# DeltaNet feeding a GELU layer pair on one core: chunk 0's state update tied to chunk 1's first joins, ScalarE's exponents, squares and scalings pinned, chunk 2's tail brought forward

## The chip, the cores and the metric

The kernel runs on one core of a Trainium2 chip. The metric is the device time of one execution in microseconds (us); smaller is better. Times inside an execution are counted from the start of the profiled span. A core has a matrix engine (TensorE, PE in the profile, with its weight loads as PEld), VectorE (DVE), ScalarE (ACT), GpSimd (POOL) and a queue of its own for issuing DMAs (SyncE, SP). Each of them works through its own list of instructions in order, and they wait for each other by semaphores.

## The reference

```python
B, H, S, D = 4, 8, 768, 48               # inputs q, k, v, beta
k_n = k / (norm(k) + 1e-06)
state = zeros(B, H, D, D)
for t in range(S):
    y[:, :, t] = q[:, :, t] @ state      # per head
    v_old = state^T k_n[:, :, t]
    state = state + beta[:, :, t] * outer(k_n[:, :, t], v[:, :, t] - v_old)
x = y.transpose(0, 2, 1, 3).reshape(B * S, H * D)     # 3072 x 384
h = x @ w_in                                          # 384 x 2048
g = 0.5 * h * (1.0 + erf(h / sqrt(2)))                # exact GELU
out = g @ w_out                                       # 2048 x 384
```

All data that is computed with is float32; the two weight matrices arrive as 64-bit floats.

## The kernel before

**Chunks.** The sequence of 768 tokens is cut into 12 chunks of 64 tokens. A chunk has two units (a = 0 and 1) of two batches each, so a unit's tokens of two batches fill the 128 partitions. Inside a chunk the recurrence is written as products of small matrices: the gram matrix of the keys (`products`, `grams`), the inverse of a triangular 64x64 matrix for each of 32 heads, computed on VectorE on 32x32 diagonal blocks by elimination (`eliminate_steps`, a chain of L443 and L445 pairs) and joined to 64x64 on TensorE in two levels (`join`, L488; VectorE's L499 writes the first level's result `XM`, ScalarE's L503 the second's), then `against_state` (L603), `solve` (L633, copied out by ScalarE's L639), `use` (L651, the outputs), `update` (L660, the new contribution to the state) and `next_state` (VectorE's L665 adds it to `St`). `read` (L672 by ScalarE for chunks 0 and 1, L674 by VectorE after) gives x, and `turn` transposes x on TensorE (L692 for chunk 1, L695 for the others) and copies it as `xT` (L696). Chunk 1's `turn` adds two parts, y and x, in PSUM. A pair of chunks shares one elimination.

**The layers.** `fc1` (L718) computes one slice f of 128 of the 2048 hidden columns for both units of a chunk, three matmuls, and ScalarE puts the GELU (L720) into `G[:, f]`. For chunks 0 and 1 `fc2` (L731) multiplies G by w_out, four slices f at a time for each unit, and the last group is followed by a copy to `o_sb` (L735) and two output DMAs issued by ScalarE (`send`, L725). From chunk 2 on the second layer takes seven products of half size (L756) with sums on VectorE (`mix`). PSUM holds four kinds of buffers: `dn` (two, of two banks each: psJ, psU, psY, psK, psG, and psH for the first eight slices of chunk 1), `mlp` (two: psH and psO), and the small pool `sq` (psT, psX and, from late in chunk 0's time, one buffer alone).

**The weights.** Each weight is a pair of 32-bit words; VectorE and ScalarE put together the 32-bit float from them, in 16 parts: 0 to 7 are w_in (256 columns, two slices f each), 8 to 15 are w_out (two rows of slices f each). A part takes `begin` on VectorE (L218, cut out the exponent), `exponents` on ScalarE (L223), `mantissas` on VectorE (L228 and L230) and `signed` on VectorE (L235 and L236), and `signed` also fetches a later part into the place that came free. Parts 0 to 2 are decoded in the section that is ordered by hand, the others by the plan.

**What sets the order.** The first part of the program, up to `by_hand.close()`, is under a manual schedule of all engines: there each engine's order is the order of the calls. It ends, for chunk 0, with the decoding of parts 0, 1 and 2 woven into `solve`, `use`, `read`, `turn`, `update` and `next_state`. What follows is a list `plan` of pairs of a due time and a function. `at(first, last, steps)` spreads steps between two due times, `emit` sorts all of them by time and calls them. The unit of due time is about one chunk: fc1 and fc2 of chunk c lie between c + 1 and c + 2 (chunk 0 to 2.25, chunk 1 from 2.25). VectorE alone keeps that order; the orders of TensorE, ScalarE, SP and GpSimd come from a scheduler that may move ready instructions around. Two helpers hold instructions in place: `tc.keep_in_program_order(i)` pins one, and `together(...)` chains the TensorE instructions of its steps to one another and to the one before, so that nothing gets between.

Around the change the plan holds: chunk 0's sixteen fc1 slices; the joins of chunk 1's units (`join(0, range(2, 4), level)`), due from 1.02 to 1.1; `sums`, 32 single-head squares with a sum (L291) for chunks 2 and 3, due from 1.08 to 1.5; the decoding of parts 3 to 15 from 0.985 to 1.65; `state_steps(1)` from 1.12 to 1.6; `scale_head` (L329, the values of chunks 2 and 3 scaled head by head on ScalarE, 32 of them) from 2.08 to 2.44; and near the end of chunk 1's layers `state_steps(2)` without its first step from 2.8 to 2.985, and the grams of chunk 4 from 2.8 to 2.9. `prep(4)` (L278, whole squares of the keys on ScalarE) is due at 2.73, and the ones of chunk 5 before 3. Loads of later chunks are issued on SP by `fetch_in` (L96) and `load_blocks` (L134, sixteen small DMAs for a chunk).

Of the kernel before, what the change touches and what calls it, by code (L numbers as in the profile page):

```python
# [12 lines left out]
ACT = mybir.ActivationFunctionType  # L13
# [3 lines left out]
def kernel(  # L17
# [28 lines left out]
    nc = tc.nc  # L46
    B, H, S, D = q.shape
    DM, DF = moe_w_in.shape
    C = 64
    HB = 32  # L50
    NC = S // C
    NP = H // 2
    NA = B // 2
# [15 lines left out]
    def dn(name):  # L69
        return ps.tile([128, 2, 512], F32, tag="dn", name=name)  # L70

    def sq(name, *shape):
        return small[0].tile([128, *shape], F32, tag="sq", name=name)
# [9 lines left out]
    lim = cpool.tile([128, 2], F32)  # L83
# [7 lines left out]
    tiles = {}  # L91
# [7 lines left out]
    for c in range(NC):  # L99
        for a in range(NA):  # L100
            u = tiles[c, a] = Unit()
# [48 lines left out]
    first = [tiles[c, a] for c in range(2) for a in range(NA)]  # L150
# [63 lines left out]
    def begin(n):  # L214
        e = su.tile([128, WG], U32, tag="w_e", name="w_e")
        raw = w_raw.pop(n)
        halves[n] = w_parts[n][0].rearrange("q m n -> q (m n)"), raw[:, :, 0], raw[:, :, 1], e
        nc.vector.tensor_scalar(e, raw[:, :, 1], 20, 0x7FF, op0=ALU.logical_shift_right,  # L218
                                op1=ALU.bitwise_and)

    def exponents(n):
        e = halves[n][3]
        nc.scalar.activation(e, e, ACT.Relu, bias=lim[:, 0:1], scale=float(2 ** 23))  # L223

    def mantissas(n):
        dst, lo, hi, e = halves[n]
        bits = dst.bitcast(U32)
        nc.vector.tensor_scalar(bits, hi, 0xFFFFF, 0x100000, op0=ALU.bitwise_and,  # L228
                                op1=ALU.bitwise_or)
        nc.vector.scalar_tensor_tensor(dst, lo, 2.0 ** -32, bits, ALU.mult, ALU.add)  # L230
# [10 lines left out]
    def decode_steps(first, last):  # L241
        def start_(n):
            begin(n)
            exponents(n)

        steps = [(0.6, start_, first), (1.5, mantissas, first)]
        for n in range(first, last):
            if n + 1 < last:
                steps += [(0.6, start_, n + 1), (1.9, signed, n), (1.5, mantissas, n + 1)]
        return steps + [(1.9, signed, last - 1)]  # L250
# [4 lines left out]
    Ds, Gs, Nus, XMs, gms, ns = {}, {}, {}, {}, {}, {}  # L255
# [27 lines left out]
    def sum_of_squares(u, h):  # L283

        if "both" not in ns:
            n23 = wk.tile([128, 2 * NA, H], F32, tag="n0", name="n0", bufs=1)
            ns[2], ns[3] = n23[:, 0:NA], n23[:, NA:]
            ns["both"] = n23
        if h == 0:
            u.ksq = wk.tile([128, H, D], F32, tag="ksq", name="ksq")  # L290
        nc.scalar.activation(u.ksq[:, h], u.Kn[:, h, 0:D], ACT.Square,  # L291
                             accum_out=ns[u.c][:, u.a, h:h + 1])

    def prep(c):
        us = [tiles[c, a] for a in range(NA)]
# [30 lines left out]
            nc.vector.scalar_tensor_tensor(x if i == 2 else s, s, 0.5, r, ALU.mult, ALU.add)  # L326

    def scale_head(u, h):
        nc.scalar.mul(u.V[:, h], u.V[:, h], ns[u.c][:, u.a, h:h + 1])  # L329

    def scale_v(u, engine=nc.gpsimd):
        engine.tensor_tensor(u.V, u.V, ns[u.c][:, u.a].unsqueeze(2).to_broadcast([128, H, D]),
                                op=ALU.mult)
# [144 lines left out]
    def join(g, ts, level, copy=nc.scalar.copy):  # L478

        xm, zf, off = XMs[g], Zf[g % 2], Gs[g]  # L480
        gm = gms[g].rearrange("q t h -> q (t h)")
        psJ = dn("psJ").rearrange("q b (u n) -> q b u n", n=HB)
        for i, u in enumerate(range(ts[0] * H, (ts[-1] + 1) * H)):
            for p in range(2):
                top = slice(p * C, p * C + HB)
                low_ = slice(p * C + HB, (p + 1) * C)
                rows, to = (top, low_) if level == 0 else (low_, top)
                nc.tensor.matmul(psJ[to, i // (2 * H), i % (2 * H), :],  # L488
                                 lhsT=(xm if level else off)[rows, u, :],
                                 rhs=zf[rows, u, HB:C] if level else xm[rows, u, :],  # L490
                                 start=True, stop=True)
        for i in range(0, len(ts), 2):
            us = slice(ts[i] * H, (ts[min(i + 1, len(ts) - 1)] + 1) * H)
            n = us.stop - us.start
            for p in range(2):
                top = slice(p * C, p * C + HB)
                low_ = slice(p * C + HB, (p + 1) * C)
                if level == 0:
                    nc.vector.tensor_tensor(  # L499
                        xm[low_, us, :], psJ[low_, i // 2, 0:n],  # L500
                        gm[low_, us].unsqueeze(2).to_broadcast([HB, n, HB]), op=ALU.mult)
                else:
                    copy(zf[top, us, HB:C], psJ[top, i // 2, 0:n])  # L503
# [70 lines left out]
    def join_steps(g):  # L574
        a, b = range(NA), range(NA, 2 * NA)
        return [(join_run, g, a, ()), (join_run, g, b, a), (join_run, g, (), b)]
# [79 lines left out]
    def update(u):  # L656
        if u.c < NC - 1:
            for j in range(NP):
                for r, p in QUADS:
                    nc.tensor.matmul(u.psS[HALF[r], p, j, :], lhsT=u.Kp[HALF[p], 2 * j + r, :],  # L660
                                     rhs=u.U[HALF[p], 2 * j + r, :], start=True, stop=True)

    def next_state(u):
        if u.c < NC - 1:
            nc.vector.tensor_tensor(St[:, u.a], St[:, u.a], u.psS, op=ALU.add)  # L665
# [32 lines left out]
    def state_steps(c, first=(), second=()):  # L698
        us = [tiles[c, a] for a in range(NA)]
        steps = [(3.0, together, (against_state, us), *first),  # L700
                 (2.0, together, (solve, us), *second), (3.0, outputs, us)]
        return steps + [(0.5, turn, u) for u in us]


# [128 lines left out]
    def ffn_steps(c):  # L833
        ones = [(1.3, fc1, c, f) for f in range(NF)]
        if c > 1:
            return [(1.3, first_layer, c, f) for f in range(NF)] + [
                (2.6, second_layer, c, n) for n in (1, 5, 2, 6, 4, 7, 3)]
        twos = [(2.7, fc2, tiles[c, a], f, f + 4) for a in range(NA) for f in range(0, NF, 4)]
        if c == 0:
            twos.sort(key=lambda s: s[3])  # L840
            more_ = [(1.3, fc1, 1, f) for f in range(EARLY)]
            return ones + twos[:-2 * NA] + more_[:4] + twos[-2 * NA:-NA] + more_[4:] + twos[-NA:]
        return ones[EARLY:] + twos

    def at(first, last, steps):

        total, done, timed = sum(s[0] for s in steps), 0.0, []
        for w, *step in steps:
            timed.append((first + (last - first) * (done + 0.5 * w) / total, step))
            done += w  # L850
        return timed
# [78 lines left out]
    clear_[0](*clear_[1:])  # L930
    for u in first[NA:]:
        scale_v(u)
    begin(0)
    exponents(0)
    mantissas(0)
    begin(1)
    mantissas(1)
    solve(first[:NA])
    exponents(1)
    signed(0)  # L940
    use(first[:NA])
    for u in first[:NA]:
# [1 line left out]
    signed(1)  # L944
    for u in first[:NA]:
        turn(u)
    for u in first[:NA]:
        update(u)
    begin(2)
    exponents(2)  # L950
    mantissas(2)
    signed(2)
    for u in first[:NA]:
        next_state(u)
    by_hand.close()
    tc.no_sync_barrier()

# [3 lines left out]
    def late():  # L961
# [3 lines left out]
        for a in range(NA):  # L965
# [3 lines left out]
            for c in range(5, NC, 2):  # L969
                tiles[c, a].Kb = Kb  # L970

    plan = [at(c + 1 + 0.25 * (c == 1), c + 2 + 0.25 * (c == 0), ffn_steps(c)) for c in range(NC)]
    plan += [at(0.985, 1.26, decode_steps(3, n_in)), at(1.26, 1.65, decode_steps(n_in, NW)), at(1.66, 1.67, [(1.0, late)])]
    rows1, join1 = eliminate_steps(1), join_steps(1)
    plan += [at(0.98, 0.985, [(1.0, load, 3)]),
             at(1.02, 1.1, [(1.0, join, 0, range(NA, 2 * NA), level) for level in range(2)]),
]
    sums = [(1.0, sum_of_squares, tiles[c, a], h) for c in (2, 3) for a in range(NA) for h in range(H)]
    plan += [at(1.08, 1.5, sums), at(1.51, 1.511, [(1.0, prep, c) for c in (2, 3)]), at(1.65, 1.655, [(1.0, finish_both)]), at(2.97, 2.971, [(1.0, finish, 4)]), at(2.725, 2.726, [(1.0, queries, third)]),
             at(1.12, 1.6, state_steps(1)),  # L980
# [4 lines left out]
             at(2.71, 2.711, [(1.0, subtract, third)]),  # L985
             at(2.7, 2.701, [(1.0, together, join1[1]), (0.0, copy_out, "join", 4)]),
             at(2.75, 2.751, [(1.0, together, join1[2]), (0.0, copy_out, "join", 4)]),
             at(2.8, 2.985, state_steps(2)[1:]),
             at(2.73, 2.731, [(1.0, prep, 4)]), at(2.8, 2.9, [(1.0, grams, [tiles[4, a] for a in range(NA)])])]
    plan += [at(0.995, 1.0, [(1.0, load_v, 2)]), at(2.98, 2.981, [(1.0, sums_of_w)]), at(3.1, 3.11, [(1.0, last_sum_of_w)])]  # L990
    plan += [at(c - 0.4, c - 0.3, v_steps(c)) for c in range(4, NC)]
    plan += [at(2.08, 2.44, [(1.0, scale_head, tiles[c, a], h)
# [2 lines left out]
    for c in range(4, NC):  # L995
        us = [tiles[c, a] for a in range(NA)]
        t = {4: 1.8, 5: 2.1}.get(c, c - 2.9)
        plan += [at(t, t + 0.01, [(1.0, load_blocks, c, "Kb", k)])]
        t = 3.2 if c == 4 else c - (1.3 if c % 2 == 0 else 0.9)
        plan += [at(t, t + 0.01, [(1.0, load_blocks, c, "Qb", q)])]  # L1000
        t = c - (2.1 if c % 2 == 0 else 2.4) if c > 5 else {4: 2.1, 5: 2.74}[c]
        plan += [at(t, t + 0.01, [(1.0, load_k, c, "Kn")])]
        plan += [at(c - 0.4, c - 0.39, [(1.0, load_k, c, "Kp")])]
        t = {4: 2.76, 5: 2.955}.get(c, c - (1.97 if c % 2 == 0 else 2.49))
        plan += [at(t, t + 0.01, [(1.0, turned_k, u) for u in us])]
        t = c + (0.05 if c % 2 == 0 else -0.34)
# [67 lines left out]
```

## Time and profile before

| | us |
|---|---|
| median of six runs | 659.95 |
| lowest and highest | 659.13, 660.38 |
| the profiled execution's own time | 659.91 |
| its span | 658.2 |
| TensorE busy in the span | 631.7 (96%) |
| VectorE busy | 456.7 (69%) |
| ScalarE busy | 230.5 (35%) |
| GpSimd busy | 80.8 (12%) |

The span is what the profiler records from the first to the last instruction; the profiled execution's own time is 1.7 us longer. In the timeline a row names the start, the duration, the engine, the line and the operation with output and input, how many instructions it stands for, and in brackets the idle time before it and who ended it. A matmul of float32 appears as two records, so the three matmuls of an fc1 slice are six records. Rows that overlap by about 0.1 us on VectorE or ScalarE are back to back: the time from one start to the next is what an operation costs there. TensorE is busy from about 60 us on nearly without a break, and the prefix before that, in which the first units are prepared, takes the rest. The granted clock of TensorE is half of full from 43.48 to 60.52 us and full after.

### The profile page before, as it was taken

What the parts mean: (1) busy time and instruction counts of PE and PEld (TensorE: products, weight loads), DVE (VectorE), ACT (ScalarE), POOL (GpSimd) and SP (SyncE); (2) the same over time, 40 slices, a digit from 0 to 9 for tenths busy, and PEclk for the clock granted to TensorE, in tenths of its full rate; (3) what the DMA queues carried; (4) which work ended last, traced back from release to release, by engine and by line L of the source; (5) the groups of instructions that cost most, each with busy time, mean ns of one, the idle gap of its engine ahead of it and who ended that gap; (6) DMA issues with size and microseconds to landing.
All of it is one profiled execution on the core that took longest, in us unless ns stands there. A gap on an engine that the chain in (4) does not pass through costs nothing.

```text
span 658.2 us, 20461 instructions
## 1 busy us (share of the span) xinstructions
PE 631.7 (96%) x8902; PEld 555.1 (84%) x8902; DVE 456.7 (69%) x941; ACT 230.5 (35%) x625; POOL 80.8 (12%) x82
## 2 busy tenths in 40 slices
PE   6767999999999999999999999999999999999997
PEld 5656777776689989989989989989989989989997
DVE  6999999987789845778845778845778844325022
ACT  3367755614342136232136132136132133131220
POOL 4041300104111011301011300011301010000000
PEclk9986999999999999999999999999999999999999
DMA  9795656302434223520323520212310210100101
GB/s 128 172 268 169 124 145 169 49 1 53 82 40 71 45 36 58 98 41 10 59 34 56 102 38 15 46 17 43 58 21 18 49 14 3 25 2 2 24 1 25
DMA packets 158426, 39.68 MB, mean 60 GB/s; under 512 B 150016, under 2 KB 153216, under 8 KB 158336
## 3 DMA queue, kind: packets, MB, share of 16 engines
q1 hardware_dynamic: 152464, 33.40, 27.0%
q10 hardware_dynamic: 5872, 4.97, 3.3%
q8 instruction: 70, 1.15, 0.7%
q14 instruction: 20, 0.16, 0.1%
HBM read 33.62 MB, written 4.72 MB: 58 GB/s over the span
## 4 chain that ended last, share of the span: by engine, by line
PE 86%; DVE 8%; ACT 2%; DMA 2%; issue 2%; SPq 0%; DVEq 0%
PE psH L718 36%; PE psX L756 12%; PE psY L756 12%; PE psO L731 5%; PE psZ L756 4%; PE psK L603 3%; PE psG L367 3%; PE psJ L529 3%; PE psU L633 2%; PE psY L651 2%; DVE Nu L445 2%; DVE tmp L443 2%; PE psY L660 1%; DMA Kp<-in_k_dram 1%; DVE w_e L235 1%
## 5 line engine op out<-in xcount | busy, mean ns | idle before, releaser
L718 PE MATMUL psH<-xT,w_in_sb 128*128 128x256 f32 x1152 | 258.9, 382 | 2.9 <-ACT G L720 2.3
L718 PEld LDWEIGHTS psH<-xT,w_in_sb 128*128 128x128 f32 x1152 | 216.5, 190 | 34.6 <-ACT G L720 3.8
L720 ACT ACTIVATE G<-psH 128x256 f32<-128x256 f32 x192 | 73.5, 383 | 179.7 <-PE psH L718 161.0
L445 DVE TENSOR_TENSOR Nu<-Nu,tmp 128x30 f32<-128x30 f32 (+9 forms) x180 | 62.4, 347 | 6.2
L443 DVE TENSOR_TENSOR tmp<-Nu 128x30 f32<-128x30 f32 (+9 forms) x180 | 60.6, 337 | 5.0
L696 ACT COPY xT<-psX 128x384 f32<-128x384 f32 x24 | 11.4, 479 | 126.8 <-PE psX L695 126.2
L756 PE MATMUL psX<-w_out_sb,G 128*128 128x192 f32 x320 | 55.8, 328 | 0.0
L756 PE MATMUL psY<-w_out_sb,G 128*128 128x192 f32 x304 | 54.1, 329 | 1.1
L756 PEld LDWEIGHTS psX<-w_out_sb,G 128*128 128x128 f32 x320 | 52.4, 190 | 0.6
L756 PEld LDWEIGHTS psY<-w_out_sb,G 128*128 128x128 f32 x304 | 49.1, 190 | 3.2 <-DVE u L802 3.2
L765 DVE TENSOR_TENSOR S<-G 128x512 f32<-128x512 f32 x20 | 13.8, 691 | 46.4 <-ACT G L720 46.2
L731 PE MATMUL psO<-w_out_sb,G 128*128 128x384 f32 x128 | 44.8, 493 | 0.0
L306 POOL TENSOR_TENSOR n<-n,half 128x16 f32<-128x16 f32 x10 | 29.4, 2940 | 123.1 <-DVE n L281 102.9
L616 DVE TENSOR_TENSOR W<-psK,V 128x384 f32<-128x384 f32 x22 | 12.2, 554 | 33.6 <-ACT y L615 33.6
L731 PEld LDWEIGHTS psO<-w_out_sb,G 128*128 128x128 f32 x128 | 23.3, 190 | 14.0 <-DVE w_out_sb L236 0.5
L639 ACT COPY U<-psU 64x192 f32<-64x192 f32 x96 | 30.1, 313 | 7.5 <-PE psU L633 6.4
L470 POOL MEMSET Zf<- 32x512 f32 x23 | 12.4, 541 | 163.4 <-DVE Zf L458 162.4
L770 DVE TENSOR_TENSOR G<-G 128x512 f32<-128x512 f32 x20 | 13.8, 692 | 25.7 <-PE psX L756 25.7
L674 DVE TENSOR_TENSOR x<-psY,y 64x192 f32<-64x192 f32 x80 | 28.3, 354 | 0.9
L756 PE MATMUL psY<-T,G 128*128 128x192 f32 x160 | 28.2, 329 | 0.0
L756 PE MATMUL psZ<-T,S 128*128 128x192 f32 x160 | 28.1, 329 | 0.0
L756 PE MATMUL psX<-T,G 128*128 128x192 f32 x160 | 28.1, 329 | 0.0
(141 smaller groups left out, 856.2 us busy)
## 6 DMA issues: line engine op xcount, KB each, us to landing
Kp<-in_k_dram SPq DMA_DIRECT2D x76, 96.0 KB, 3.3
w_out_sb<-in_moe_w_in_dram SPq DMA_DIRECT2D x24, 256.0 KB, 4.2
V<-in_v_dram SPq DMA_DIRECT2D x48, 96.0 KB, 3.4
out_dram<-o_sb ACTq DMA_DIRECT2D x46, 96.0 KB, 2.2
w_raw<-in_moe_w_out_dram SPq DMA_DIRECT2D x10, 384.0 KB, 7.3
Zf<-in_moe_w_out_dram SPq DMA_DIRECT2D x6, 384.0 KB, 3.7
Qp<-in_q_dram SPq DMA_DIRECT2D x64, 32.0 KB, 2.2
Qp<-in_q_dram SPq DMA_DIRECT2D x16, 96.0 KB, 4.2
```

Source lines behind the costliest of these rows:

```text
L306: nc.gpsimd.tensor_tensor(flat, flat, half, op=ALU.pow)
L367: nc.tensor.matmul(psG[HALF[p], r, i * NP + j, :], lhsT=u.Kt[rows, p, j, :], rhs=(u.Qt if x else u.Kt)[rows, p, j, :], start=True, stop=True)
L443: nc.vector.tensor_tensor(tmp, nu[:, j + 1:, j:j + 1].to_broadcast([128, n, j]), nu[:, j:j + 1, 0:j].to_broadcast([128, n, j]), op=ALU.mult)
L445: nc.vector.tensor_tensor(nu[:, j + 1:, 0:j], nu[:, j + 1:, 0:j], tmp, op=ALU.add)
L529: nc.tensor.matmul(psJ[HALF[p], k, :], lhsT=(xm if level else off)[rows, us, :], rhs=zf[rows, us, HB:C] if level else xm[rows, us, :], sta ...
L603: nc.tensor.matmul(u.psK[to, x, r, j, :], lhsT=(u.Qt if x else u.Kt)[rows, p, j, :], rhs=St[rows, u.a, p, j, :], start=True, stop=True)
L639: copy(pairs(u.U[HALF[p]], s), u.psU[HALF[p ^ s], p])
L674: nc.vector.tensor_tensor(dst, src, pairs(u.y[HALF[p ^ s]], s), op=ALU.add)
L718: nc.tensor.matmul(psH, lhsT=w_in_sb[:, f // 2, m, f % 2 * 128:(f % 2 + 1) * 128], rhs=xTs[c][:, m, :], start=(m == 0), stop=(m == NM - 1))
L720: nc.scalar.activation(G[:, f, :], psH, ACT.Gelu)
L731: nc.tensor.matmul(u.psO, lhsT=G[:, f, u.a * 128:(u.a + 1) * 128], rhs=w_out_sb[:, f, :], start=(f == 0), stop=(f == NF - 1))
L756: nc.tensor.matmul(ps_, lhsT=lhs[:, f, :], rhs=rhs[:, f, :], start=first and f == 0, stop=f == FH - 1, skip_group_check=not first)
```

## The change

The exponents of parts 3 and 4, the single-head squares and the scalings of single heads are pinned in ScalarE's program order. In the section by hand the decoding of parts 0 and 1 is regrouped: both `begin`, then both `exponents`, then both `mantissas`, all ahead of `solve`. `update` and `next_state` of chunk 0 leave that section and go into the plan, behind chunk 0's first fc1 slices: the updates are tied on TensorE to the first level of chunk 1's joins, and the two `next_state` and the load of chunk 3 follow. The first three slices of fc1 get due times of their own, and the second level of the joins is due at 1.1. Joins of a group's second chunk take their PSUM from the small pool, and `join` does the lower half of the partitions first. `outputs` of chunk 1 is tied together. At the end of chunk 1's layers the steps of `state_steps(2)` get due times one by one (2.79, 2.86, 2.93 and 2.95), and the grams of chunk 4 stand at 2.87.

```diff
     def exponents(n):
         e = halves[n][3]
-        nc.scalar.activation(e, e, ACT.Relu, bias=lim[:, 0:1], scale=float(2 ** 23))
+        i = nc.scalar.activation(e, e, ACT.Relu, bias=lim[:, 0:1], scale=float(2 ** 23))
+        if n in (3, 4):
+            tc.keep_in_program_order(i)
...
-        nc.scalar.activation(u.ksq[:, h], u.Kn[:, h, 0:D], ACT.Square,
-                             accum_out=ns[u.c][:, u.a, h:h + 1])
+        tc.keep_in_program_order(nc.scalar.activation(
+            u.ksq[:, h], u.Kn[:, h, 0:D], ACT.Square, accum_out=ns[u.c][:, u.a, h:h + 1]))
...
     def scale_head(u, h):
-        nc.scalar.mul(u.V[:, h], u.V[:, h], ns[u.c][:, u.a, h:h + 1])
+        tc.keep_in_program_order(
+            nc.scalar.mul(u.V[:, h], u.V[:, h], ns[u.c][:, u.a, h:h + 1]))
...
-        psJ = dn("psJ").rearrange("q b (u n) -> q b u n", n=HB)
+        psJ = dn("psJ") if ts[0] == 0 else sq("psJ", 1, 512)
+        psJ = psJ.rearrange("q b (u n) -> q b u n", n=HB)
         for i, u in enumerate(range(ts[0] * H, (ts[-1] + 1) * H)):
-            for p in range(2):
+            for p in (1, 0):
...
-                 (2.0, together, (solve, us), *second), (3.0, outputs, us)]
+                 (2.0, together, (solve, us), *second),
+                 (3.0, together, (outputs, us)) if c == 1 else (3.0, outputs, us)]
...
-    begin(0)
-    exponents(0)
-    mantissas(0)
-    begin(1)
-    mantissas(1)
+    for n in range(2):
+        begin(n)
+    for n in range(2):
+        exponents(n)
+    for n in range(2):
+        mantissas(n)
     solve(first[:NA])
-    exponents(1)
     signed(0)
...
-    for u in first[:NA]:
-        update(u)
     begin(2)
     exponents(2)
     mantissas(2)
     signed(2)
-    for u in first[:NA]:
-        next_state(u)
...
+    plan[0][:3] = at(0.97, 0.98, [s_ for s_ in ffn_steps(0)[:1]]) + at(0.986, 1.02, ffn_steps(0)[1:3])
...
-    plan += [at(0.98, 0.985, [(1.0, load, 3)]),
-             at(1.02, 1.1, [(1.0, join, 0, range(NA, 2 * NA), level) for level in range(2)]),
-]
+    b = range(NA, 2 * NA)
+    plan += [at(1.05, 1.051, [(1.0, together, *[(update, u) for u in first[:NA]], (join, 0, b, 0))]
+                + [(1.0, next_state, u) for u in first[:NA]] + [(1.0, load, 3)]),
+             at(1.1, 1.101, [(1.0, together, (join, 0, b, 1))])]
...
-             at(2.8, 2.985, state_steps(2)[1:]),
-             at(2.73, 2.731, [(1.0, prep, 4)]), at(2.8, 2.9, [(1.0, grams, [tiles[4, a] for a in range(NA)])])]
+             *[at(t, t + 0.001, [s_]) for t, s_ in zip((2.79, 2.86, 2.93, 2.95), state_steps(2)[1:])],
+             at(2.73, 2.731, [(1.0, prep, 4)]), at(2.87, 2.871, [(1.0, grams, [tiles[4, a] for a in range(NA)])])]
```

## The prediction

> **What bounds the kernel now.** I read the page first, then the waits of TensorE, then the chain of work around the end of the weight decoding, then timelines of single engines.
>
> ```profile
> PE 631.7 (96%) x8902; PEld 555.1 (84%) x8902; DVE 456.7 (69%) x941; ACT 230.5 (35%) x625; POOL 80.8 (12%) x82
> PEclk9986999999999999999999999999999999999999
> PE 86%; DVE 8%; ACT 2%; DMA 2%; issue 2%; SPq 0%; DVEq 0%
> ```
>
> TensorE is busy for 96% and makes 86% of the chain; the 8% of VectorE must lie somewhere in particular. The waits of TensorE from 60 us to the end (total, times, longest) show how little there is to win:
>
> ```profile
> PE psH L718 <- ACT G L720: 2.3, 3, 1.4
> PE psH L718 <- ACT xT L696: 0.6, 1, 0.6
> PE psX L695 <- DVE x L674: 0.3, 1, 0.3
> PE psT L346 <- ACT Qt L347: 0.2, 1, 0.2
> ```
>
> Together with three more lines of 0.2 to 0.3 us this is some 4.2 us. But two of these places don't count alike. The windows table gives VectorE 29.89 us of work in the 31 us from 76 to 107, and the chain there runs through its decoding of w_out (start, duration):
>
> ```profile
> 100.35 0.96 DVE w_out_sb L236
> 101.31 0.47 DVE St L665
> 101.81 0.31 ACT x L672
> ...
> 103.15 2.69 PE psX L692 x20
> 105.84 1.29 PE psO L731 x4
> ```
>
> So until 101.31 us, when VectorE has decoded part 11 (w_out rows for f = 6 and 7), VectorE is the bound: a TensorE wait before that is hidden, and a VectorE wait is paid in full. From 103.15 to 169 us TensorE runs without a break; from there every TensorE microsecond is paid. The two VectorE waits before 101 us total 0.7:
>
> ```profile
> 59.19 0.96 DVE L235 SCALAR_TENSOR_TENSOR w_e<-w_out_sb,w_e 128x768 uint32<-128x768 uint32 x1 [0.35 <-ACT w_e L223]
> 87.97 0.96 DVE L235 SCALAR_TENSOR_TENSOR w_e<-Zf,w_e 128x768 uint32<-128x768 uint32 x1 [0.39 <-ACT w_e L223]
> ```
>
> Both wait for an exponent pass (L223) that ScalarE had behind other copies.
>
> **What the Trainium skill says.** "TensorE: Matmul & The Clock Gate", Part 1: TensorE's clock is halved after an idle window and restored after a busy one; the window is 3413 ns and free-running. The trace agrees in length: granted 0.5 from 43.48 to 60.52 us, 17.04 us, five windows. The same page, "Architectural detail": ScalarE and VectorE queues are strictly first in, first out. Here a GELU whose matmul was done stands behind a square that waits for a DMA (below). "SBUF — State Buffer", "two separate sides": a VectorE operation with two SBUF inputs, or in its fast mode, and a GpSimd operation lock each other out. Here L228 takes 0.56 us alone and 1.19 beside a GpSimd multiply, L230 0.96 and 1.47. "DMA: Bandwidth & Descriptors", anatomy: waits are made by the issuing sequencer, not by the DMA engines; so a blocked SP issue holds all later loads, as it does at 160 to 175 us here.
>
> **The change part by part**, in the order of time. I took the changed order from the two built programs.
>
> 1. Exponents by hand. Exponents of part 1 (0.84 from start to start) now run before the U copies, not between them and the x copies; so both xT copies come 0.84 earlier (the second at 57.0 instead of 57.84), and exponents of part 2 no longer wait behind them. VectorE's L235 would follow L230 after 0.88 as at 54.08 to 54.96, instead of 1.31 (57.88 to 59.19): −0.43. Against it, begin of part 1 moves ahead of mantissas of part 0, so two mantissa passes instead of one can meet the GpSimd multiply: up to 0.6+0.5, of which one pair is already paid; I take +0.2 (bounds 0 and +1.1). Nearest row: L228 at 50.49.
>
> 2. Update of chunk 0 (64 matmuls, 1.96 us on the slow clock) goes behind fc1 f0 to f2. TensorE does the same work in another order: f0 at 57.49 cold (2.56) to 60.05, then warm 1.295 each, f2 done 62.88, update 0.94 to 63.8, first join 1.1 to 64.9. VectorE's XM (L499, 1.41) has its slot at about 65.0 to 65.2 in the changed order, since St (2×0.94) now follows it: just in time. St after XM is the same 1.9 us. Cost 0, hidden by 0.1 to 0.3 us of cover; without the cover see rival A. That psJ takes a bank of the small pool removes the wait of the join for St, 0.2, which is hidden anyway. The load of chunk 3 goes later and part 7's fetch earlier on SP; part 7 is decoded after 80 us: 0. GpSimd's queue keeps its order.
>
> 3. ScalarE's order to 101 us. Exponents 3 and 4 are pinned ahead of GELUs; squares are spread to about 104 us. Exponents of part 8 now precede the chunk-1 U copies (8×0.32): L235 at 87.97 comes 0.48 earlier (87.02 to 87.97 is 0.95, unwaited 0.47). TensorE in exchange waits at f10 and f14, 1 to 1.5 us each, for GELUs behind exponents and four squares. TensorE reaches the w_out matmuls of f6 about 2 us before VectorE's part 11 even so: 0. The order also lets two PSUM-reading St follow other work: −0.1. Sum of VectorE gains: 0.43+0.48+0.1−0.2 = −0.8 (bounds −1.2 and 0).
>
> 4. End of chunk 1. Before, part 11 ready (101.31) is followed by St, four x copies and then X: 0.5+1.3+0.04, X 2.53, two w_out matmuls 1.29, next fc1 at 106.97, that is 5.66 later. After, three w_out matmuls (0.645 each) stand between part 11 and X, and three behind it: 0.05+1.94+2.53+1.94 = 6.46. +0.8 (bounds +0.8, and 0 if the three run before part 11 because TensorE is not late). With step 3 the start of chunk 1's fc1 stays where it is, bounds −1.2 and +0.8. I take −0.2: if part 11 comes 0.8 sooner, TensorE may be a little late for it, and one of the three then runs before it is needed.
>
> 5. V scalings (L329, 0.225 apart), pinned in program order. The piece of ScalarE before:
>
> ```profile
> 127.42 0.56 ACT L329 ACTIVATE V<-V,n 128x48 f32<-128x48 f32 x2 [1.03 <-issue]
> 127.89 0.46 ACT L735 COPY o_sb<-psO 128x384 f32<-128x384 f32 x1
> 128.38 1.12 ACTq L725 DMA_DIRECT2D out_dram<-o_sb  x2
> 129.55 0.39 ACT L720 ACTIVATE G<-psH 128x256 f32<-128x256 f32 x1 [1.20 <-PE psH L718]
> ```
>
> The GELU of f8 is released by the two DMA issues, 7.06 us after the last w_out group began (122.49), is done at 7.45, and f10 needs its buffer at 7.75: 0.3 to spare. After, five scalings stand between the two copies and four behind the last issues. Copy 2.7 to 3.17, issues to 4.39, 5×0.225 to 5.56, copy to 6.02, issues to 7.17, 4×0.225 to 8.1, GELU to 8.5: f10 waits 0.8 where nothing follows to take it up. +0.8 (bounds 0, if the copies start early, and +1.0). Later slices carry three scalings each: 0.38+0.68 is under 1.295.
>
> 6. Tail of chunk 2. Outputs come ahead of the grams and are cut apart by w_out matmuls. Removed: 0.54 before X a (0.27 shown), 0.73 before fc1 (0.62 shown). Added: grams wait for x, some 0.35. That is −0.9. But:
>
> ```profile
> 170.78 4.73 SPq L96 DMA_DIRECT2D Kp<-in_k_dram  x7
> 177.30 0.52 ACT L278 ACTIVATE ksq<-Kp 128x384 f32<-128x384 f32 x1 [1.08 <-DMA Kp<-in_k_dram]
> 178.62 0.66 PE L346 MATMUL psT<-ident,Qp 128*128 128x128 f32 x4 [0.22 <-ACT Qt L347]
> ```
>
> The square at 177.30 waits for a K load that SP issued at about 173.5 us, after 16 Qp loads (10.06) and Kp loads in an unbroken run from 159.93. That run starts when ScalarE reads an earlier K tile at 159.38, which the edit doesn't move. Behind the square stand the GELU of f2 and the Qt copy, and TensorE's second transposes wait for that copy. So TensorE arrives 0.9 us sooner and waits 0.9 more: 0 net (bounds −0.9, and 0). That two Qt copies precede the second square takes off at most the 0.22.
>
> Sum: −0.2+0.8+0 = +0.6. The profiled run is 659.91 (span 658.2 and 1.7 around it), 0.04 under the median 659.95 of six; so 660.5 against either.
>
> **The rivals.**
>
> A, slower: TensorE's clock stays low one window longer. In the window 57.11 to 60.52 TensorE was full before and was granted full speed at its end; now it starts at 57.49, 89% full. If that isn't enough (the window before it, with 1.03+0.41 idle, 58%, was not), the low clock lasts to 63.93: f1 and f2 cost 2.56, the join ends at about 66.6, and VectorE, which has XM next at 65.1, stands 1.5 still on the path that sets the end. It decides from the moment when the join ends after 65.2. 660.5+1.5 = 662.0. For it: the cover is 0.1 to 0.3 us. Against: 89% is near the full window.
>
> B, faster: the K load comes earlier than I think, and scalings find room in ScalarE's idle time (it is busy 17.07 of 33 us from 107 to 140). For it: both stalls removed in step 6 are real. Against: the unbroken run of SP, and that scalings are in program order. Then −0.2−0.9+0 = −1.1: 658.8.
>
> C, the scalings find room (step 5 at 0), but the tail gives its gain back: −0.2, 659.7; no change that can be told. For and against it as for the two halves of B.
>
> **How the numbers follow.** About 0.2%, 1.3 us, is what a measurement here can tell from no change: 658.6 and 661.3. Forecast with its neighbourhood (659.8 to 661.3) 0.47; A 0.2; B 0.15; C 0.18. Faster: most of B, 0.1, and 0.03 of bounds below C, 0.13. Slower: A's 0.2 and 0.06 of the forecast's upper bounds, 0.26. Same: 0.61. The range reaches from B's 658.8, with 0.1 left out below, to 662.2, just above A, with 0.1 left out above.
>
> **What would show it.** Right: L235 of parts 2 and 8 without a wait; the last L236 of part 11 0.5 to 1.2 us earlier than 101.31; chunk 1's first late fc1 some 6.4 us behind it, three w_out matmuls ahead of X; a wait psH←G of about 0.8 near 131 us; no wait of X and fc1 at 169 to 173, but a longer one at psT before 179. Wrong: the clock at full speed only from 63.9 (A); the square at 177.30 without its wait on Kp (B); f10 of chunk 1 without a wait (B, C); a VectorE wait at XM near 65 us.

## The result, and the profile after

| | before | after |
|---|---|---|
| median us (runs) | 659.81 (38) | 661.42 (18) |
| lowest, highest | 658.96, 661.15 | 659.57, 662.74 |
| profiled execution's own time | 659.91 | 661.89 |
| its span | 658.2 | 660.1 |

The ratio is 1.0023, with a 95% interval from 1.0017 to 1.0030: 1.5 us slower, from 1.1 to 2.0. The forecast was 660.5, 0.6 above before; the range holds the result, and the excess of 0.9 has to be found. By the prediction's own limit of 1.3 us the result is just on the slower side, to which it gave 0.26, and 661.4 lies nearer to rival A's 662.0 than to 660.5.

The waits of TensorE in the changed kernel, from 60 us to the end (total, times, longest), and below them the only wait of VectorE from 40 to 110:

```profile
PE psH L723 <- ACT G L725: 2.7, 3, 1.4
PE psO L736 <- DVE w_out_sb L238: 1.4, 1, 1.4
PE psT L349 <- ACT Qt L350: 1.2, 1, 1.2
PE psG L370 <- issue: 0.4, 1, 0.4
PE psG L370 <- DVE x L678: 0.4, 1, 0.4
```

```profile
DVE XM L503 <- PE psJ L492: 0.7, 1, 0.7
```

The two waits of VectorE for exponents are gone and there is one for the first join instead. TensorE's waits for xT and x in the tail are gone; there is a larger one for Qt, and two at the grams. Lines have moved by up to five: L235 and L236 of before are L237 and L238, L720 is L725.

The absolute times of two executions can't be set side by side here. The first exponent cut of the weight decoding on VectorE (L218), which nothing of the change precedes, began at 47.69 us in the profile before and at 47.17 after, and at 46.7 to 47.7 in the other profiles of this study. I count from there:

| counted from that instruction, us | before | after |
|---|---|---|
| first join of chunk 1's units ends (L488, now L492) | 15.29 | 18.32 |
| part 11 decoded (end of its L236, now L238) | 53.62 | 53.35 |
| chunk 1's fc1 begins again | 59.28 | 59.66 |
| from there to the end of the span | 551.23 | 553.27 |

0.38 is lost ahead of chunk 1's late fc1 and 2.04 behind it. (Less the 0.52 by which the common instruction came earlier, that is the 1.9 between the two spans; the profiled execution after is 0.47 above its median, the one before 0.10.) Two timelines show the second piece. ScalarE at the end of the first w_out groups of chunk 1:

```profile
128.01 0.46 ACT L740 COPY o_sb<-psO 128x384 f32<-128x384 f32 x1
128.50 1.12 ACTq L730 DMA_DIRECT2D out_dram<-o_sb  x2
129.67 1.01 ACT L332 ACTIVATE V<-V,n 128x48 f32<-128x48 f32 x4 [1.20 <-issue]
130.59 0.36 ACT L725 ACTIVATE G<-psH 128x256 f32<-128x256 f32 x1
```

And TensorE, at the same place and in the tail of chunk 2, with ScalarE's square behind which it stands:

```profile
131.00 1.35 PE L723 MATMUL psH<-xT,w_in_sb 128*128 128x256 f32 x5 [0.74 <-ACT G L725]
...
166.59 0.93 PE L370 MATMUL psG<-Kt 48*64 48x64 f32 x48 [0.36 <-DVE x L678]
167.96 0.46 PE L370 MATMUL psG<-Kt 48*64 48x64 f32 x16 [0.44 <-issue]
...
173.78 4.05 PE L723 MATMUL psH<-xT,w_in_sb 128*128 128x256 f32 x18
180.33 0.66 PE L349 MATMUL psT<-ident,Qp 128*128 128x128 f32 x4 [1.20 <-ACT Qt L350]
```

```profile
179.00 0.52 ACT L280 ACTIVATE ksq<-Kp 128x384 f32<-128x384 f32 x1 [2.05 <-DMA Kp<-in_k_dram]
```

The four scalings stand between the DMA issues and the GELU of f8, and f10 waits. Counted from chunk 1's late fc1, f10 begins 24.17 us later, against 23.27 before: 0.9. In the tail fc1 of chunk 2 begins 66.95 us after it, against 65.97: still 1.0 behind, so the tail's new order has won nothing up to there. The fc1 behind the grams of chunk 5 (182.00 and 180.30) stands at 75.17 against 73.33: the wait for Qt has put 0.86 on top. So the 2.04 are 1.0 at the scalings, 0.84 in the tail and 0.2 behind it.

Where the prediction had TensorE come sooner to that wait, the K load came later instead. SP's run of sixteen loads ahead of it, before and after:

```profile
160.62 10.06 SPq L134 DMA_DIRECT2D Qp<-in_k_dram  x16
```

```profile
161.48 10.59 SPq L134 DMA_DIRECT2D Qp<-in_k_dram  x16
```

The run was 0.53 longer and the load landed another 0.3 later behind it. In the fourteen profiles of this study the run takes 9.5 to 10.6 us, so a part of the 0.84 may be this execution's own.

### The profile page after: what moved, and what is told of

Its sections match the earlier page's. It is cut to its first block, busy times and chain, and to the rows that moved or that the text cites. A ratio compares the mean times of both kernels' runs of the same rounds, so it can differ in the third digit from the quotient of the medians.

```text
span 660.1 us, 20469 instructions
## 1 busy us (share of the span) xinstructions
PE 632.8 (96%) x8902; PEld 555.7 (84%) x8902; DVE 457.4 (69%) x941; ACT 231.3 (35%) x625; POOL 80.9 (12%) x82
## 3 DMA queue, kind: packets, MB, share of 16 engines
q8 instruction: 70, 1.15, 0.7%
## 4 chain that ended last, share of the span: by engine, by line
PE 85%; DVE 10%; ACT 2%; issue 2%; DMA 1%; ACTq 1%; SPq 0%; DVEq 0%
PE psH L723 35%; PE psX L761 12%; PE psY L761 12%; PE psO L736 5%; PE psZ L761 4%; PE psK L607 3%; PE psG L370 3%; PE psJ L533 2%; PE psU L637 2%; PE psY L655 2%; DVE tmp L446 2%; DVE Nu L448 2%; PE psY L664 1%; DMA Kp<-in_k_dram 1%; DVE w_e L237 1%
## 5 line engine op out<-in xcount | busy, mean ns | idle before, releaser
L725 ACT ACTIVATE G<-psH 128x256 f32<-128x256 f32 x192 | 73.5, 384 | 180.0 <-PE psH L723 162.9
L545 DVE TENSOR_TENSOR XM<-psJ,gm 32x256 f32<-32x256 f32 x40 | 16.8, 421 | 16.8 <-PE psJ L533 16.2
```

The lines of the kernel that those rows point to most:

```text
L545: nc.vector.tensor_tensor(xm[low_, us, :], src, gm[low_, us].unsqueeze(2).to_broadcast([HB, H, HB]), op=ALU.mult)
L725: nc.scalar.activation(G[:, f, :], psH, ACT.Gelu)
```

## The experiments

My theory after this reading: four independent terms, the order of the first layer (with its w_out order), the scalings, the tail, and the square that stands before a GELU and two Qt copies in the tail. The rival: all of the loss is the first layer's, in one mechanism (the low clock), and the rest is hidden somewhere. Every experiment is compared with the kernel before on the same chip; its median lay between 658.99 and 659.7 there.

**The scalings alone.** The kernel before with

```diff
     def scale_head(u, h):
-        nc.scalar.mul(u.V[:, h], u.V[:, h], ns[u.c][:, u.a, h:h + 1])
+        tc.keep_in_program_order(
+            nc.scalar.mul(u.V[:, h], u.V[:, h], ns[u.c][:, u.a, h:h + 1]))
```

> The kernel before, with only the scalings of single heads pinned in ScalarE's order. Theory (the scalings make a new wait at f10 of chunk 1, with nothing after it to take it up): +0.8 to +0.9 us, 660.6 to 660.7, and a wait of psH for G near 131 us. Rival (ScalarE is half idle from 107 to 140 us and takes the scalings without delay): no change, 659.8.

Measured: 660.15 against 659.3, ratio 1.0014 (1.0007 to 1.0020), +0.9. TensorE's timeline names the place:

```profile
127.00 2.75 PE L719 MATMUL psH<-xT,w_in_sb 128*128 128x256 f32 x12
130.49 3.72 PE L719 MATMUL psH<-xT,w_in_sb 128*128 128x256 f32 x16 [0.74 <-ACT G L721]
```

One wait at f10, as forecast. ScalarE's idle time doesn't help, since the pins put the scalings into the only stretch where it is on the path.

**The tail alone.** The kernel before with the change's due times for `state_steps(2)` and for the grams of chunk 4, nothing else.

```diff
-             at(2.8, 2.985, state_steps(2)[1:]),
+             *[at(t, t + 0.001, [s_]) for t, s_ in zip((2.79, 2.86, 2.93, 2.95), state_steps(2)[1:])],
...
-             ... at(2.8, 2.9, [(1.0, grams, [tiles[4, a] for a in range(NA)])])]
+             ... at(2.87, 2.871, [(1.0, grams, [tiles[4, a] for a in range(NA)])])]
```

> The kernel before, with only the due times of chunk 2's tail and of the grams of chunk 4 changed. Theory (what the new order removes before the transposes and before fc1 comes back at the grams and at the wait for a Qt copy that stands behind a square waiting for its load): between 0 and +0.5 us. Rival (the stalls at 169 to 173 us are gone for good): -0.9 us, 658.9.

Measured: 659.61 against 659.3, ratio 1.0003 (0.9995 to 1.0011), +0.2 with an interval that holds zero. TensorE's waits from 140 to 185 us:

```profile
PE psT L346 <- ACT Qt L347: 0.8, 1, 0.8
PE psG L367 <- DVE x L674: 0.4, 1, 0.4
PE psG L367 <- issue: 0.3, 1, 0.3
```

What is removed at the transposes stands at the grams and at psT, all in sight.

**The square away, in the changed kernel.** The square that waits at 179.00 is chunk 6's, which the plan calls only at 4.59; the scheduler has moved it to where its keys have not yet come. I pinned it:

```diff
         if engine is None:
-            nc.scalar.activation(ksq, kd, ACT.Square)
+            i = nc.scalar.activation(ksq, kd, ACT.Square)
+            if u.c == 6:
+                tc.keep_in_program_order(i)
```

> The changed kernel, with the whole squares of chunk 6's keys pinned in ScalarE's program order, so that they run after 190 us and not at 179 in front of a GELU and of two Qt copies. Theory: the 1.2 us wait of the second Qp transposes goes, -1.2 us against the changed kernel, 660.2. Rival (something else holds the transposes or the grams behind them): 661.4 as the changed kernel.

Measured: 659.75 against 659.3 of before, ratio 1.0005 (0.9997 to 1.0013). The changed kernel stood at 1.0023 in its own set of runs, so by the two ratios the edit takes off 1.2 us. ScalarE there now, without an idle stretch for a DMA:

```profile
175.46 0.38 ACT L727 ACTIVATE G<-psH 128x256 f32<-128x256 f32 x1 [0.43 <-PE psH L725]
176.76 0.38 ACT L727 ACTIVATE G<-psH 128x256 f32<-128x256 f32 x1 [0.91 <-PE psH L725]
177.19 0.58 ACT L352 COPY Qt<-psT 128x512 f32<-128x512 f32 x1
```

**Tail and square in the kernel before.** The last two edits together.

> The kernel before, with the new tail and with chunk 6's squares pinned as well. Theory (the new tail removes nothing that it doesn't add at the grams; only the square's wait, 0.2 to 0.4 us in the kernel before, goes): -0.3 us, 659.5. Rival (the tail's gain of 0.9 us was there and was only given back to the square): -1.2 us, 658.6.

Measured: 658.32 against 659.3, ratio 0.9985 (0.9979 to 0.9992), -1.0. My theory of that run is refuted, and the rival's number is nearly met. From the second `solve` of the tail (L633) to fc1 it took 14.35 us before, 14.22 with the tail alone and 13.96 here: the order is worth 0.4 here, where the grams show no second stop by "issue". The other 0.5 to 0.6 is the square. But the stop is smaller here rather than gone:

```profile
164.97 1.47 PE L369 MATMUL psG<-Kt 48*64 48x64 f32 x64 [0.36 <-DVE x L676]
```

From the start of these 64 grams to the next w_out matmul it took 1.76 us in the changed kernel, 1.66 with the tail alone, 1.40 here and 1.10 before.

**The square alone, in the kernel before.**

> The kernel before, with chunk 6's whole squares pinned in ScalarE's program order and nothing else. It shows how much of the last run's 1.0 us is the square alone. Theory (the tail's order is worth about 0.4 and the square the rest in that run, but in the kernel before the square holds the second transposes by 0.4 only): -0.4 us. Rival (the square alone makes the whole gain, the tail's order none): -1.0 us.

Measured: 658.89 against 659.7, ratio 0.9990 (0.9982 to 0.9998), -0.7. It lies between the two numbers; what is sure is that the square cost something before the change too, and that the tail's order adds some tenths once it is out of the way.

**The first part, as one piece.** All edits up to the transposes of chunk 1, without the scalings' pins and the tail.

> All edits of the change up to the end of chunk 1's transposes (regrouping, pins of exponents and squares, update tied with the joins, joins in the small pool, outputs of chunk 1 tied), with the scalings and the tail as before. Theory (VectorE's gain of 0.8 is paid back by the three w_out matmuls in front of the transposes and the third one behind): chunk 1's late fc1 at 106.8 instead of 107.0, -0.1 to -0.2 us. Rival (the first layer's new order is itself the loss): +0.5 us or more.

Measured: 660.06 against 659.7, ratio 1.0004 (0.9995 to 1.0012), +0.3. But the thirteen runs are spread from 658.58 to 660.78, five under 659.2 and eight over 659.9, where the kernel before, on the same chip, lies between 658.52 and 660.42 without such a gap. The unpinned square widens the times too, so kernels have to be compared that have it alike: with it pinned, the standard deviation is 0.24 to 0.35 us in three kernels with the old first layer (before_ksq, before_tail_ksq, hand_tail_ksq) and 0.59 with the new one (after_ksq); unpinned it is 0.43 before and 0.83 here. The profiled execution was of the good kind (658.7). Its clock and its join show why, the windows (length, TensorE busy, clock granted, DMA share, GB/s) first for the changed kernel and then for this one:

```profile
60.00:61.00 1.00, 1.00 (x3) 0.50 0.42 102
61.00:62.00 1.00, 1.00 (x5) 0.85 0.64 215
```

```profile
58.00:60.00 2.00, 2.00 (x6) 0.51 0.83 298
60.00:61.00 1.00, 1.00 (x6) 1.00 0.75 207
```

The mean of 0.85 in the second says that the clock was low until 61.30 (0.30 at 0.5 and 0.70 at 1); here it was low until 59.96. The same kind of fc1 work, f0 to f2, took 6.25 us after and 5.65 here, and VectorE's instruction for the join reads, after and here:

```profile
65.53 1.40 DVE L503 TENSOR_TENSOR XM<-psJ,gm 32x512 f32<-32x512 f32 x2 [0.68 <-PE psJ L492]
```

```profile
64.80 1.39 DVE L502 TENSOR_TENSOR XM<-psJ,gm 32x512 f32<-32x512 f32 x2
```

Counted from the first decoding step, for three profiles with the new first layer and two with the old one:

| kernel | clock rises | join ends | VectorE waits for it | part 11 decoded | late fc1 |
|---|---|---|---|---|---|
| before | 12.85 | 15.29 | 0 | 53.62 | 59.28 |
| before_ksq | 15.77 | 16.59 | 0 | 54.00 | 59.66 |
| before_first_part | 12.91 | 17.71 | 0 | 52.74 | 59.04 |
| after_ksq | 13.30 | 17.89 | 0.27 | 52.89 | 59.19 |
| after | 14.13 | 18.32 | 0.68 | 53.35 | 59.66 |

From the third row to the fifth the clock rises 1.22 later and the join ends 0.61 later: half, because the work between runs at half speed. And the wait of VectorE passes on, 0.68 against 0.61 at part 11 and 0.62 at fc1. The shorter wait of after_ksq passed on 0.15 of its 0.27. In the old order the join is done 1.1 to 3.0 us earlier, and a rise at 15.77 costs no wait for psJ (before_ksq is 0.4 late at part 11, but its only waits of VectorE are one of 0.6 for a DMA and one of 0.7 for exponents, against 0.7 in all before). The clock's rise differs from one execution to the next by at least 3 us (12.7 to 15.8 in fourteen profiles), which no edit explains: before and before_ksq have the same program up to there. The stretches of low clock that end with this rise last 13.65, 17.07, 20.48 or 23.89 us, always a multiple of 3.41, and the rise came at the end of a 3.41 that TensorE had filled: with 3.01 us of work in it the clock stayed low (six profiles), with 3.06 it rose (this one). The 89% of rival A, 3.03 us, lies right at that limit.

**The regrouping of parts 0 and 1 alone.** Both begins, both exponents, both mantissas ahead of `solve`.

> The kernel before, with only the decoding of parts 0 and 1 regrouped in the section by hand (both begins, both exponents, both mantissas ahead of the solve). Theory (VectorE is the bound to 101 us, exponents of part 2 come in time): the L235 at 59 us without a wait, the last L236 of part 11 0.43 us earlier, and -0.4 us. Rival (the gain goes to a GpSimd multiply that the second mantissas meet, or TensorE is the bound there): no change.

Measured: 659.24 against 659.7, ratio 0.9996 (0.9987 to 1.0004): not to be told from nothing. The trace is plainer. The wait at 59 us is gone, and yet that L235 begins 11.47 us after the first decoding step, and 11.50 before: nothing is won. The begin of part 1 now runs beside a memset of GpSimd (L470) and takes 0.97 us instead of 0.56, so that parts 0 and 1 are done 0.41 later. The begin of part 1 before, and both begins here:

```profile
50.02 0.56 DVE L218 TENSOR_SCALAR w_e<-w_out_sb 128x768 uint32<-128x768 uint32 x1
```

```profile
47.71 1.43 DVE L218 TENSOR_SCALAR w_e<-w_out_sb 128x768 uint32<-128x768 uint32 x2
```

In all eight profiles with the regrouping this L235 stands at 11.47 or 11.48. The run's rival had GpSimd as the taker, at its multiply. At part 8 stands

```profile
87.95 0.96 DVE L235 SCALAR_TENSOR_TENSOR w_e<-Zf,w_e 128x768 uint32<-128x768 uint32 x1 [0.58 <-ACT w_e L223]
```

that is 40.24 us from the first decoding step, and 40.28 before. What VectorE wins between the two parts in this execution, 0.2 at shorter waits, goes to a longer wait for the exponents of part 8, because ScalarE has these behind the U copies of chunk 1, which follow TensorE and not VectorE.

**The regrouping with the pins of exponents and squares.**

> The same regrouping, and the exponents of parts 3 and 4 and the single-head squares pinned as in the changed kernel; update and joins of the first layer stay as before, and so does TensorE's order at the end of chunk 1. Theory (VectorE gains 0.43 at part 2 and 0.48 at part 8, and nothing is paid for TensorE's order): -0.8 to -0.9 us. Rival (the waits of TensorE for GELUs behind squares make it late for part 11): -0.4 or less.

Measured: 660.95 against 659.7, ratio 1.0025 (1.0015 to 1.0035), +1.3 where I expected -0.8. One line shows where:

```profile
88.89 0.96 DVE L237 SCALAR_TENSOR_TENSOR w_e<-Zf,w_e 128x768 uint32<-128x768 uint32 x1 [2.25 <-ACT w_e L223]
```

That is 41.89 from the first step, 1.6 later than before, and part 11 and the late fc1 are 1.6 and 1.7 later as well. ScalarE's U copies begin 37.11 after the first step here, 36.15 before and 35.24 in the changed kernel, and the exponents stand behind them and behind pinned squares. Of the 1.6 the U copies make 1.0 and the squares 0.7 (the exponents begin 3.82 after the first copy, 3.16 before).

The U copies may be late by chance. This execution is one of the slower of nine (661.83; they lie between 660.29 and 662.42), and in it the clock was low once more, from 68.28 to 71.70 us. Three fc1 slices took 5.79 us there instead of 3.9:

```profile
68.35 5.79 PE L720 MATMUL psH<-xT,w_in_sb 128*128 128x256 f32 x18
```

No other of the fourteen profiles has this second stretch, which takes 1.7 us from TensorE. So the pins with the regrouping are a loss, since even the fastest of the nine is 0.6 above the median before; how much of it is theirs without that stretch, the trace doesn't tell. In the changed kernel the first layer's new order brings TensorE, the U copies and with them these exponents forward by 0.9, and L237 at 87.14 us runs without a wait.

**The update and the joins alone.** The reverse: only the move of `update`, `next_state` and the joins.

> The kernel before, with only the update of chunk 0 and the joins moved and tied as in the changed kernel (with the small pool's psJ and the halves exchanged); exponents and pins as before. x is 0.85 us later here than in the changed kernel, VectorE's own order only 0.44. Theory (VectorE waits for the join): 1.2 us of waiting in the mean and 0.6 for the order of the w_out matmuls: +1.3 to +1.9 us, psJ named as VectorE's wait. Rival (the move by itself is harmless): +0.3 or less.

Measured: 662.69 against 658.99, ratio 1.0061 (1.0049 to 1.0073), +3.7, twice what I expected. VectorE, and below it TensorE:

```profile
68.12 1.40 DVE L500 TENSOR_TENSOR XM<-psJ,gm 32x512 f32<-32x512 f32 x2 [3.27 <-PE psJ L489]
```

```profile
64.31 1.56 PE L719 MATMUL psH<-xT,w_in_sb 128*128 128x256 f32 x6 [1.52 <-ACT G L721]
66.88 1.20 PE L489 MATMUL psJ<-XM,G 32*32 32x32 f32 x64
```

I had counted the later x and the late clock. The rest is a GELU behind two unpinned exponent passes and five unpinned squares, 1.52, which now lies in front of the join because f2 does. So the pins are needed by the move as much as the move by the pins: +1.3 (pins and regrouping) and +3.7 apart, +0.3 together. Which of the pins it is, exponents or squares, was not run.

**Filling TensorE ahead of the first layer.** If the low clock in front of the join is the trouble, more work in TensorE's gaps should raise it sooner.

```diff
     signed(1)
-    for u in first[:NA]:
+    warm = sq("warm", NM, 128)
+    for u, n in zip(first[:NA], (1, 2)):
+        for i in range(n):
+            nc.tensor.transpose(warm[:, 0, :], ident, ident)
         turn(u)
+    for i in range(2):
+        nc.tensor.transpose(warm[:, 0, :], ident, ident)
```

> The kernel of the run before_first_part with five more transposes of the identity on TensorE (one ahead of the first, two ahead of the second group of x transposes of chunk 0, two ahead of fc1), into a PSUM tile that nobody reads; they fill TensorE's gaps at 53 to 57 us and change no other order. Theory (in the new order the join stands behind fc1 f0 to f2 on the low clock, whose end depends on where the clock's window falls, so that VectorE waits for psJ between 0 and 1.7 us, 0.84 in the mean): the clock rises up to one window earlier, VectorE never waits, times come to lie within about 1 us instead of 2.2, and the median is 0.6 to 0.8 below before_first_part: -0.4 us against the kernel before. Rival (the spread and the +0.3 of before_first_part come from elsewhere): +0.3 us as there, same spread.

Measured: 660.61 against 658.99, ratio 1.0025 (1.0015 to 1.0035), +1.6: a loss, and the remedy doesn't work. TensorE:

```profile
54.93 0.63 PE L952 MATMUL warm<-ident 128*128 128x128 f32 x2
56.05 0.90 PE L698 MATMUL psX<-ident,x 128*128 128x128 f32 x3 [0.49 <-ACT xT L699]
56.74 0.64 PE L955 MATMUL warm<-ident 128*128 128x128 f32 x2
```

The unread tile holds one of the pool's two buffers, so that the second group of transposes waits for the first xT copy: fc1 began 10.34 after the first decoding step, 9.85 in before_first_part. The clock rose at 13.48, no sooner, the join ended at 18.23 and VectorE waited 0.61. That a later join is paid by VectorE is seen once more. That filling raises the clock earlier is not seen, but it isn't settled: 13.48 here and 12.99 in the other kernel with the filling, against 12.91 to 14.13 in the three without, are few draws. Its loss against before_first_part (1.3) is more than the 0.5 by which fc1 is late. The rest lies far behind, in a join that no edit touches:

```profile
446.87 0.27 PE L532 MATMUL psJ<-Zf,XM 32*64 32x64 f32 x2 [0.64 <-issue]
```

From the start of this join to the next fc1 it takes 1.99 us here and 1.08 in before_first_part. The other kernel with the filling stops at the same place (0.74), the twelve without it don't.

**Two combinations.** The regrouping, the tail and the square in the kernel before:

> The kernel before with the three parts that have been found harmless or good one by one: decoding of parts 0 and 1 regrouped, the new tail, chunk 6's squares pinned. If they add up: -0.4 and -1.0, -1.4 us. If VectorE's 0.43 is lost as soon as TensorE is ahead: -1.0.

Measured: 658.40 against 658.99, ratio 0.9990 (0.9984 to 0.9997), -0.6. Not -1.4: the regrouping adds nothing, as its own run has shown. The whole change without the scalings' pins, with the square pinned and the filling:

> The whole change without the pins of the scalings, with chunk 6's squares pinned and the five filling transposes. If the parts add up: -0.4 (first part, filled) and -1.0 (tail and square): -1.4 us against the kernel before. If the filling does nothing: -0.7.

Measured: 659.79 against 658.99, ratio 1.0015 (1.0007 to 1.0023), +0.8: the filled first part's +1.6 less the 0.7 to 1.0 of tail and square. The version that beats both kernels is before_tail_ksq, the kernel before with the new tail and the square pinned, at 0.9985.

## Why the prediction came out as it did

The direction and the range hold; the sum of 0.6 was 0.9 short. Two terms that it put at zero were not zero, the join in step 2 and, in the changed kernel, the tail in step 6; and VectorE's gain (steps 1 and 3) came out partly by luck. Against its steps:

- **Step 1, regrouping (-0.43 + 0.2): failed.** The wait at part 2 went, but GpSimd took the gain: 0.41 at its memset, beside the begin of part 1, where the prediction had looked at its multiply and put 0.2. L235 of part 2 begins 0.03 earlier instead of 0.23.
- **Step 2, update behind f0 to f2 (0, covered by 0.1 to 0.3 us): failed.** The cover depends on when the clock rises, which differs by 3 us between executions; at half speed that moves the join's end by 1.5. VectorE waited 0, 0.27 and 0.68 us in three executions, of which 0, 0.15 and 0.61 reached part 11. A wait of VectorE at XM near 65 us was on the prediction's own list of signs that it is wrong. Rival A had the mechanism and the price of an uncovered join, but took it as one case that happens or not (a fuller window) where it is spread over the executions. An estimate: the rise can't come much before the 12.91 of before_first_part, since TensorE is full only from 9.85; if it then falls anywhere in 3.41, it is 1.7 later in the mean, the join 0.85. By its own run the first part is 0.5 above the forecast (+0.3 for -0.2), with an interval from -0.3 to +0.8; the wider times of the new first layer agree with a wait that comes and goes, but its mean is not measured.
- **Step 3, ScalarE's order to 101 us (part of -0.8): the sum right, partly by luck.** Without VectorE's wait part 11 came 52.74 after the first step, 0.88 sooner. Part 8 gave 0.48 and the order of St 0.12, as written; part 2 gave 0.03, and 0.28 came from short waits between parts 5 and 6, which the prediction hadn't counted. Nor do the exponents of part 8 precede the U copies as I wrote; they come in time since the copies are 0.9 earlier.
- **Step 4, w_out order (+0.8): right.** Part 11 to fc1 took 6.30 where 6.46 was worked out, and 5.66 before: +0.64. Steps 1 to 4 together without a wait for the join give -0.24 at fc1 (59.04 against 59.28) in the one trace of that kind, where I had -0.2.
- **Step 5, scalings (+0.8): right.** +0.9, alone and within the change, and at the place named.
- **Step 6, tail (0 net): failed in the changed kernel.** Alone the tail costs 0.2 with an interval from -0.3 to +0.7, which doesn't exclude zero; in the changed kernel's trace it loses 0.84. The term that was mis-sized is the grams' wait, put at 0.35. The order was to gain 0.9; it gained 0.02 in the changed kernel, 0.13 alone, and 0.4 to 0.6 in the four kernels that have it with the square pinned. The give-back at psT has the size written, 0.86, but by luck: TensorE did not come sooner, the K load came later. That SP's loads set it was right; that the wait can be had by pinning one square, the prediction didn't see, and the square is there two chunks before it is needed. Pinning it took 1.2 off the changed kernel and 0.7 off the one before.

The parts, each by its own run: +0.3 (first part), +0.9 (scalings), +0.2 (tail), sum 1.4, against 1.5 measured. Each is known to 0.4 or 0.5 only, so the sum fits but doesn't show that the parts add up. The changed kernel's trace puts 0.4 on the first part, 1.0 on the scalings and 0.8 on the tail, in an execution above the median.

"TensorE: Matmul & The Clock Gate", Part 1 of the Trainium skill, calls the clock's window free-running, and I had quoted that. Its consequence was in front of me: what a run of the kernel before shows (60.5 us) is one draw. The runs agree with it, 12.7 to 15.8 us being a span of 3.1 and the window 3.4 by the page. The rule I had quoted beside it, half clock after an idle window, is too narrow by these runs: in before_hand_exp_sq the clock fell after 3.41 us in which TensorE was busy for 1.62.

What stays open: what TensorE's stops by "issue" are. They stand in front of the last grams in the changed kernel and with the tail alone (0.4 and 0.3 us). In the four kernels with the tail and the pinned square nothing is named there, but these grams take 1.15 to 1.40 us to the next matmul, 1.10 before. With the filling a stop stands in a join 390 us behind the edit. Nothing in the traces names the cause, and no run was made for it.

## What to carry to other kernels

Where work on a low clock is moved in front of something that a full engine waits for, count its time for the latest rise of the clock, not for the one that the profile at hand happened to show. An engine that is nearly always busy may still have waits that aren't its own to win: follow each to the engine that feeds it, and look at what the moved instruction will then run beside, since the wait may go and its time be lost elsewhere. And compare two traces from a common instruction, because the stretch ahead of the change moved by up to a microsecond here between executions of equal code.

## What the runs showed of the hardware

The rise of TensorE's clock fell between 12.7 and 15.8 us after the same instruction in fourteen executions, and at 12.85 and 15.77 in two programs that are equal up to it. The low stretches were multiples of 3.41 us. A 3.41 with 3.01 us of TensorE's work left the clock low, one with 3.06 raised it; at full clock one with 1.62 lowered it (before_hand_exp_sq) and one with 1.89 didn't (before_update). Two DMA issues on ScalarE took 1.12 to 1.25 us in the changed kernel, and ScalarE did no arithmetic for as long, which is what made the scalings behind them so dear. VectorE's L218 over 128x768 took 0.54 and 0.97 us in before_hand, the second beside a memset of GpSimd.
